# Moving T's copies to ScalarE and v's to VectorE in a fused FFT, soft-MoE and MLP kernel

## Chip, cores and metric

The kernel runs on one core of a Trainium2 chip. The metric is the device time of one execution in microseconds; the time of a kernel is the median of its runs.

## What is computed

The input x is 8 images of 3072 x 256. The reference takes the real part of a two-dimensional Fourier transform of each, flattens the images to 24576 rows, passes them through a soft mixture of 8 experts with 4 slots each, and then through a two-layer network.

```python
X = np.fft.fft(np.fft.fft(x, axis=1), axis=2).real
logits = x @ phi
d = softmax over the rows of logits
slot_out = relu((d.T @ x)[e] @ w1[e]) @ w2[e]
c = softmax over the slots of logits
x = c @ slot_out
h = x @ w_in
out = (s * relu(h)**2 + b) @ w_out
```

w_in and w_out arrive as float64 and are converted on the chip.

## The kernel before, in words

An image of 3072 rows is called a batch, and comes as three pages of 1,024 KB (`xb`), x0, x2 and x1, loaded in that order by `load_x` (L280). Pages of this size come from a ring of 15 (`page`), which later holds everything else that is large: the pages `xrt` of x for the weighted sums, tables (`ltab`, `htab_t`), logits (`lg`), raw and converted weights (`raw`, `wo`, `wi`, `whl`), `w1t` and `w2t`. A load waits until the last reader of the page it takes over is done. All loads are issued by SyncE in program order, so one that waits holds up those behind it.

The program is written for a manual schedule: each engine runs its instructions in the order in which the Python code emits them.

The first stage never forms the full transform. For each batch it computes V, x times a projected phi, transposed back, and then T, V times a 128-point table.
- `project` (L498) makes the projected phi, `phd`.
- `fold(b, op)` (L391) uses the symmetry of the transform: VectorE subtracts the mirrored page x2 from x0 into a page `fd`, and later adds it to x0 in place (L400, two instructions each). ScalarE copies one row that has no mirror (L395).
- `emit_v(n)` (L402): n = 2b is the even V, from x0 and `fd`, in 8 narrow matmuls (L413); n = 2b + 1 is the odd V, from x1 and x2, unfolded (L428). ScalarE copies V out of PSUM into `vts` (L419, L437). The last batch has an unfolded even V.
- `turn_v(n)` transposes it into `vq` (L446), and `turned_out(n)` copies that into `v` (L454): the even half by VectorE, the odd half by ScalarE.
- `emit_t(b)` (L458) multiplies v of one batch with the table into `tps` (L488) and puts eight small copies of it to `tt` on the list `late_t` (L496). For most batches six are ScalarE's and two VectorE's.

The loop over seven batches (L510) does, for batch b: start loads of x; fold (subtract); turned_out of batch b - 1; fold (add); odd V; T of batch b - 1; even V; all copies in `late_t`; transposes. The eighth batch follows, unfolded.

After the loop, `ORDER` (L287) gives the loads of a table in DRAM (s), x pages for the sums (r), and pages for tables (l, h). Then come the logits (L602), their exponentials and a second transform (L677), and the stage of weighted sums (L753 on TensorE), in which VectorE also converts w_out and w_in, four chunks each, in five steps per chunk (`double_steps`, L151 to L165), a maximum (L214, L231) and a split (L208). A raw page is free after the fifth step (L165). A string at L838 sets the order of the loads of x pages (x), w_out chunks (o) and w_in chunks (i). The experts follow (L962, L994), and then the two-layer network (L1158 to L1195), most of the run.

Of the kernel before, what the change touches and what calls it, by code (L numbers as in the profile page):

```python
# [13 lines left out]
ALU = mybir.AluOpType  # L14
# [19 lines left out]
def tile_fft2__then__softmoe__then__act_relu2(  # L34
# [18 lines left out]
    nc = tc.nc  # L53
    P = 128
    NS1 = 24
    B, S, D = 8, NS1 * P, xp.shape[-1]
# [40 lines left out]
    def page(shape, dt, name, among=9):  # L97
        k = [k for k, p in enumerate(pools[:among]) if p[2] < p[1]][-(len(pools) == 4)]
        pools[k][2] += 1
        return pools[k][0].tile(shape, dt, tag="page", name=name), k  # L100
# [4 lines left out]
    def drop(k):  # L105
        pools[k][2] -= 1
# [10 lines left out]
    def busy(eng, cost, after=0.0):  # L117
        at[eng] = max(at[eng], after, at["pe"]) + cost
# [165 lines left out]
    NX = 3 * B  # L284
    CR, BUDGET = 0.5, 3.9
    LEAD, TOL, LT, LX, HX = 14.0, 0.5, 0, 0, 1
    ORDER = 20 * "x" + "srllhh"  # L287
    tpool = tc.alloc_tile_pool(name="tpool", bufs=1)
    order = list(ORDER)

# [83 lines left out]
    with tc.tile_pool(name="xtp", bufs=1, side="right") as xtp, tc.tile_pool(name="vp", bufs=1, side="right") as vp, \  # L374
# [6 lines left out]
        late_t = []  # L381

        def turned(n, c, i, k, rev):

            v = xa[n][0][:, c, i, P - 1:P] if rev else xa[n][0][:, c, i, 0:1]
            sg = -1 if rev else 1
            return bass.AP(tensor=v.tensor, offset=v.offset, ap=[list(v.ap[0]), [sg * 2 * P, k], [sg, P]])

        fds = {}

        def fold(b, op):  # L391
            x0, x2 = xa[3 * b][0], xa[3 * b + 1][0]
            if op == ALU.subtract:
                fds[b] = page([P, 2, 8, P], F32, "fd")
                nc.scalar.copy(fds[b][0][:, :, 0, :], x0[:, :, 0, :])  # L395
            for c in range(2):
                v = x2[:, c, 7, P - 1:P]
                r = bass.AP(tensor=v.tensor, offset=v.offset, ap=[list(v.ap[0]), [-P, 7], [-1, P]])
                a = x0[:, c, 1:8, :]
                nc.vector.tensor_tensor(out=fds[b][0][:, c, 1:8, :] if op == ALU.subtract else a, in0=a, in1=r, op=op)  # L400

        def emit_v(n):  # L402
            b, part = divmod(n, 2)
            x0, x2, x1 = 3 * b, 3 * b + 1, 3 * b + 2
            vt = psv.tile([P, 4, P], F32, name="vt", bufs=2)

            if part == 0 and b < B - 1:
                d, dk = fds.pop(b)
                for c in range(2):
                    for h in range(2):  # L410
                        for j, t in enumerate((xa[x0][0], d)):
                            q = 64 * h + NE * j
                            nc.tensor.matmul(vt[q:q + NE], lhsT=phd[:, c, 0, NE * j:NE * j + NE], rhs=t[:, c, h::2, :],  # L413
                                             start=(c == 0), stop=(c == 1), tile_position=(0, q), skip_group_check=True)
                at["pe"] = max(at["pe"], x_at[x2] + 4.5) + 1.9
                for k in (xa[x0][1], dk):
                    drop(k)
                vts[n] = xtp.tile([P, 4, P], F32, name="vts", bufs=2)
                nc.scalar.copy(vts[n], vt)  # L419
                return  # L420
            if part == 0:
                todo_v = [(0, 0, 0, x0, 0, 4, 0), (1, 0, 0, x0, 1, 4, 0), (0, 1, 1, x2, 6, 3, 1), (1, 1, 0, x2, 7, 4, 1)]
            else:
                todo_v = [(0, 0, 0, x1, 0, 3, 0), (1, 0, 0, x1, 1, 3, 0), (0, 1, 0, x2, 0, 1, 1), (1, 1, 0, x1, 7, 2, 1),
                          (0, 1, 1, x1, 6, 1, 1)]
            for c in range(2):
                for m, (h, sg, o, pg, i, k, rev) in enumerate(todo_v):
                    nc.tensor.matmul(vt[64 * h:64 * h + 64, o:o + k, :], lhsT=phd[:, c, sg, :],  # L428
                                     rhs=turned(pg, c, i, k, rev), start=(c == 0 and m < 2), stop=(c == 1 and m >= len(todo_v) - 2),
                                     tile_position=(0, 64 * h), skip_group_check=True)  # L430
            at["pe"] = max(at["pe"], x_at[x1 if part else x2]) + (2.3 if part else 3.6)
            for pg in ((x1, x2) if part else (x0,)):
                drop(xa[pg][1])
            busy("act", 0.5)
            ns = 3 if part else 4
            vts[n] = xtp.tile([P, 4, P], F32, name="vts", bufs=2)
            (nc.scalar.copy if n < 2 * B - 1 else nc.vector.tensor_copy)(vts[n][:, 0:ns], vt[:, 0:ns])  # L437
# [11 lines left out]
        def turned_out(n):  # L449
            b, part = divmod(n, 2)  # L450
            bg, bq = divmod(b, NG)
            nk = 10 if part else 16
            vq = vqs.pop(n)
            (nc.scalar.copy if part and n < 2 * B - 4 else nc.vector.tensor_copy)(  # L454
                vs[bg][:, bq, :, 16 * part:16 * part + nk].rearrange("p (k j) n -> p j k n", j=4),
                vq.rearrange("p s (k j e) -> p j e (s k)", j=4, e=8)[:, :, :, 0:nk])

        def emit_t(b):  # L458
# [32 lines left out]
            for j in range(4):  # L491
                for c in range(2):
                    r = 64 * bg + NR * c
                    args = (tt[r:r + NR, :, bq, 8 * j:8 * j + 8],
                            t[NR * j:NR * j + NR, :, 64 * c:64 * c + 64].rearrange("p e k -> p k e"))
                    late_t.append(lambda args=args, dve=2 * j + c > 5 - b // (B - 2): (nc.vector.tensor_copy if dve else nc.scalar.copy)(*args))  # L496

        def project():  # L498
            pp = psv.tile([P, 2, 2, NE], F32, tag="tps", name="pp", bufs=2)
# [9 lines left out]

        for b in range(B - 1):  # L510
            pump_a()
            fold(b, ALU.subtract)
            if b:
                for n in range(2 * b - 2, 2 * b):
                    turned_out(n)
            fold(b, ALU.add)
            emit_v(2 * b + 1)
            if b:
                emit_t(b - 1)
            emit_v(2 * b)  # L520
            while late_t:
                late_t.pop(0)()
            turn_v(2 * b + 1)
            turn_v(2 * b)
            if b == 0:
                tp = psv.tile([P, P], F32, tag="tps", name="tp", bufs=2)
                nc.tensor.transpose(tp, f_sb, ident)
                nc.vector.tensor_copy(ft_sb, tp)
        for n in range(2 * B - 4, 2 * B - 2):
            turned_out(n)  # L530
        emit_v(2 * B - 2)
        while order:
            order_step()
        emit_t(B - 2)
# [300 lines left out]
        nc.sync.dma_start(out=w2t[e][:, c], in_=w2[e].rearrange("(p c) d -> p c d", p=P)[:, c])  # L835

    loads = {"o": iter(range(4)), "i": iter(range(4))}
    for c in "oxxoxxoxxoxxixxixxixix":  # L838
        if c == "x":
            todo.append((1, load_xr))  # L840
        else:
            k = next(loads[c])
            todo.append((3 - 2 * (k % 2), lambda k=k: wo_load(k), 1 - k % 2) if c == "o" else
                        (2 - k % 2, lambda k=k: wi_load(k), 1 - k % 2))
# [510 lines left out]
```

## Time and profile before

| | |
|---|---|
| median of 3 runs | 1443.61 us (1443.05 to 1444.81) |
| the profiled execution | 1445.31 us |
| its span | 1443.5 us |
| TensorE busy | 1374.8 us (95%) |
| VectorE busy | 1207.4 us (84%) |
| ScalarE busy | 1007.3 us (70%) |
| GpSimd busy | 237.0 us (16%) |
| DMA queue of the loads and stores | 110.78 MB |

The span is what the trace covers; the 1.8 us between it and the execution's own time lie around it. TensorE's 95% is an average over stages: of the 40 slices of the span, the first seven or so belong to the stages ahead of the two-layer network, and there its busy tenths are 6 to 9, with the granted clock at 7 to 9 tenths. A busy share says little about which engine sets the pace, so the rows to look at are those that tell what an engine waited for.

### The profile page before, as it was taken

How to read it: one execution, taken by the hardware profiler on the slowest of the kernel's cores; microseconds unless marked ns; L12 is line 12 of the kernel's file. 1: busy time of each engine (PE TensorE's matmuls, PEld its weight loads, DVE VectorE, ACT ScalarE, POOL GpSimd, SP SyncE). 2: the span in 40 equal slices, each digit the busy share in tenths (PEclk: the TensorE clock that was granted, in tenths of full speed). 3: DMA queues.
4: the chain of work that ended last, by engine and by line, in shares of the span. 5: the costliest groups of instructions: out<-in, count | busy, mean ns of one | idle time of the engine just before them, and what ended most of it. 6: DMA issues, size and time to landing. Idle time of an engine off the chain costs nothing.

```text
span 1443.5 us, 23041 instructions
## 1 busy us (share of the span) xinstructions
PE 1374.8 (95%) x8990; PEld 836.1 (58%) x8990; DVE 1207.4 (84%) x1523; ACT 1007.3 (70%) x1423; POOL 237.0 (16%) x287
## 2 busy tenths in 40 slices
PE   6667986999999999999999999999999999999998
PEld 4435653556666666666666666666666666666665
DVE  3446797599898989898989898989898989888886
ACT  2235431588787777787777787877777777777775
POOL 0030360012121212121212121111111111111110
PEclk8789997999999999999999999999999999999999
DMA  9955598210101010101010101010101010101001
GB/s 386 405 190 189 196 405 332 87 36 22 36 23 35 23 35 23 36 22 36 23 35 22 33 23 35 23 36 23 35 23 36 23 36 22 35 22 34 23 23 30
DMA packets 72460, 112.27 MB, mean 78 GB/s; under 512 B 34096, under 2 KB 59696, under 8 KB 64928
## 3 DMA queue, kind: packets, MB, share of 16 engines
q1 hardware_dynamic: 72320, 110.78, 22.3%
q8 instruction: 70, 1.15, 0.3%
q14 instruction: 38, 0.31, 0.1%
q0 software_dynamic: 32, 0.03, 0.0%
HBM read 78.50 MB, written 26.21 MB: 73 GB/s over the span
## 4 chain that ended last, share of the span: by engine, by line
PE 87%; DVE 7%; ACT 2%; issue 1%; DMA 1%; SPq 1%; POOL 0%; ACTq 0%; DVEq 0%; POOLq 0%
PE op L1192 45%; PE op L1195 23%; PE fhp L1158 11%; PE tps L488 2%; ACT tt L496 2%; PE vt L413 1%; DVE fd L400 1%; PE hp L677 1%; DVE whl L208 1%; DMA xb<-in_x_turned_dram 1%; PE ehp L962 1%; PE eop L994 1%; DVE tt L496 1%; SPq L1121 0%; DVE cm L615 0%
## 5 line engine op out<-in xcount | busy, mean ns | idle before, releaser
L1192 PE MATMUL op<-whl,rhl 128*128 128x512 f16 x3056 | 1020.7, 379 | 0.8 <-ACT rhl L1148 0.6
L1195 PE MATMUL op<-whl,rhl 128*128 128x256 f16 x3056 | 831.4, 273 | 0.0
L1163 ACT ACTIVATE r<-fhp,wsc 128x768 f32<-128x768 f32 (+1 forms) x513 | 461.4, 900 | 230.4 <-PE fhp L1158 229.2
L1164 DVE SCALAR_TENSOR_TENSOR r<-fhp,r 128x768 f32<-128x768 f32 (+1 forms) x513 | 489.1, 954 | 113.6 <-ACT r L1163 103.6
L1149 DVE TENSOR_TENSOR rhl<-r,rhl 128x768 f16<-128x768 f32 x511 | 506.8, 992 | 0.9 <-ACT rhl L1148 0.9
L1192 PEld LDWEIGHTS <-rhl 128*128 128x128 f16 x3056 | 298.9, 98 | 332.2 <-ACT rhl L1148 0.9
L1148 ACT CAST rhl<-r 128x768 f16<-128x768 f32 x511 | 420.2, 822 | 1.8 <-DVE r L1164 1.8
L1195 PEld LDWEIGHTS <-rhl 128*128 128x128 f16 x3056 | 299.0, 98 | 62.5 <-issue 0.3
L1211 POOL TENSOR_TENSOR ot<-ot,bias 128x256 f32<-128x256 f32 x189 | 137.7, 729 | 974.6 <-DVE ot L1209 974.6
L1158 PE MATMUL fhp<-ct,g 128*128 128x384 f16 x1024 | 250.5, 326 | 1.2 <-DMA g<-gs 0.8
L1158 PEld LDWEIGHTS <-g 128*128 128x128 f16 x1024 | 99.9, 98 | 69.0 <-issue 1.5
L1208 ACT ACTIVATE o<-op,small 128x256 f32<-128x256 f32 x189 | 89.8, 476 | 16.8 <-PE op L1195 16.8
L1209 DVE SCALAR_TENSOR_TENSOR ot<-op,small,o 128x256 f32<-128x256 f32 x191 | 91.2, 478 | 0.3
L496 DVE COPY tt<-tps 32x512 f32<-32x512 f32 x15 | 10.4, 694 | 53.2 <-ACT tt L496 53.1
L488 PE MATMUL tps<-f_sb,v 128*128 128x128 f32 x112 | 22.7, 386 | 29.6 <-DVE v L454 29.6
L753 PE MATMUL racc<-xrt,dh 128*64 128x256 f32 x384 | 45.8, 392 | 0.4 <-DVE dh L743 0.4
L419 ACT COPY vts<-vt 128x512 f32<-128x512 f32 x7 | 4.1, 585 | 56.3 <-PE vt L413 56.3
L753 PEld LDWEIGHTS racc<-xrt,dh 128*64 128x64 f32 x384 | 27.1, 140 | 21.7 <-issue 6.8
L488 PEld LDWEIGHTS tps<-f_sb,v 128*128 128x128 f32 x112 | 21.1, 290 | 31.8 <-issue 29.0
L428 PE MATMUL vt<-xb,phd 128*64 128x384 f32 (+3 forms) x176 | 24.8, 430 | 3.5 <-DMA xb<-in_x_turned_dram 3.5
L800 POOL TENSOR_TENSOR lg<-lg,rm 112x512 f32<-112x512 f32 x16 | 24.7, 1545 | 11.8 <-DVE rm L798 11.8
L496 ACT COPY tt<-tps 32x512 f32<-32x512 f32 x41 | 23.6, 575 | 3.7 <-PE tps L488 3.2
(249 smaller groups left out, 592.5 us busy)
## 6 DMA issues: line engine op xcount, KB each, us to landing
xb<-in_x_turned_dram SPq DMA_DIRECT2D x24, 1024.0 KB, 19.9
xrt<-in_x_pages_dram SPq DMA_DIRECT2D x24, 1024.0 KB, 8.3
out_dram<-ot SPq DMA_DIRECT2D x128, 128.0 KB, 1.7
w1t<-in_moe_w_dram SPq DMA_DIRECT2D x8, 1024.0 KB, 8.7
out_dram<-ot SPq DMA_DIRECT2D x128, 64.0 KB, 2.0
raw<-in_moe_w_out_dram SPq DMA_DIRECT2D x4, 1024.0 KB, 8.8
raw<-in_moe_w_in_dram SPq DMA_DIRECT2D x4, 1024.0 KB, 11.8
w2t<-in_moe_w_dram SPq DMA_DIRECT2D x4, 1024.0 KB, 13.8
```

Of the source, the lines that this page charges most:

```text
L496: late_t.append(lambda args=args, dve=2 * j + c > 5 - b // (B - 2): (nc.vector.tensor_copy if dve else nc.scalar.copy)(*args))
L753: nc.tensor.matmul(raccs[acc][64 * h:64 * h + 64, :], lhsT=dh[:, m, g].rearrange("p j e -> p (j e)"), rhs=xr[k][0][:, g, t, :], start=(sum ...
L1148: nc.scalar.copy(a, r2)
L1149: nc.vector.tensor_tensor(out=l, in0=r2, in1=a, op=ALU.subtract)
L1158: nc.tensor.matmul(hp[k * split][:, k, :].rearrange("p (s b m) -> p s b m", s=2, b=B), lhsT=g16[:, f * P:(f + 1) * P], rhs=c, start=True, ...
L1163: nc.scalar.activation(out=r[:, k], in_=hp[i][:, k], func=AF.Relu, scale=wsc[:, 2, p:p + 1])
L1164: nc.vector.scalar_tensor_tensor(out=r2[:, k], in0=hp[i][:, k], scalar=0.0, in1=r[:, k], op0=ALU.max, op1=ALU.mult)
L1192: nc.tensor.matmul(op.rearrange("p h d -> p (h d)"), lhsT=a, rhs=w.rearrange("p h d -> p (h d)"), start=(f == 0), stop=False)
L1195: nc.tensor.matmul(op[:, 0, :], lhsT=l, rhs=w[:, 0, :], start=False, stop=(f == NFC - 1))
L1208: nc.scalar.activation(out=o1, in_=op[:, 1, :], func=AF.Copy, scale=qv)
L1209: nc.vector.scalar_tensor_tensor(out=ot, in0=op[:, 0, :], scalar=qv, in1=o1, op0=ALU.mult, op1=ALU.add)
L1211: nc.gpsimd.tensor_tensor(out=ot, in0=ot, in1=bias, op=ALU.add)
```

## The change

Six things change, all ahead of the two-layer network.
- T's eight copies are all ScalarE's. They run in two groups of four: the first after the even V of the batch in which T is made, the second after the odd V of the next.
- Both halves of v are copied by VectorE.
- The row without a mirror is copied into `fd` by GpSimd, not ScalarE.
- Batch 0 is not folded; its even V is projected like the last batch's, and comes before its odd V.
- One more x page is loaded ahead of the table page (r twice in `ORDER`).
- In the string of loads, the first w_out chunk comes two x pages later, and the x pages between the w_in chunks are spread.

```diff
-    ORDER = 20 * "x" + "srllhh"
+    ORDER = 20 * "x" + "srrllhh"
...
             if op == ALU.subtract:
                 fds[b] = page([P, 2, 8, P], F32, "fd")
-                nc.scalar.copy(fds[b][0][:, :, 0, :], x0[:, :, 0, :])
+                nc.gpsimd.tensor_copy(fds[b][0][:, :, 0, :], x0[:, :, 0, :])
...
-            if part == 0 and b < B - 1:
+            if part == 0 and 0 < b < B - 1:
                 d, dk = fds.pop(b)
...
-            (nc.scalar.copy if part and n < 2 * B - 4 else nc.vector.tensor_copy)(
+            nc.vector.tensor_copy(
                 vs[bg][:, bq, :, 16 * part:16 * part + nk].rearrange("p (k j) n -> p j k n", j=4),
...
-                    late_t.append(lambda args=args, dve=2 * j + c > 5 - b // (B - 2): (nc.vector.tensor_copy if dve else nc.scalar.copy)(*args))
+                    late_t.append(lambda args=args: nc.scalar.copy(*args))
...
         for b in range(B - 1):
             pump_a()
-            fold(b, ALU.subtract)
             if b:
+                fold(b, ALU.subtract)
                 for n in range(2 * b - 2, 2 * b):
                     turned_out(n)
-            fold(b, ALU.add)
+                fold(b, ALU.add)
+            else:
+                emit_v(0)
             emit_v(2 * b + 1)
+            while late_t:
+                late_t.pop(0)()
             if b:
                 emit_t(b - 1)
-            emit_v(2 * b)
-            while late_t:
+                emit_v(2 * b)
+            for _ in range(4 * (b > 0)):
                 late_t.pop(0)()
             turn_v(2 * b + 1)
             turn_v(2 * b)
...
         emit_v(2 * B - 2)
+        while late_t:
+            late_t.pop(0)()
         while order:
             order_step()
...
-    for c in "oxxoxxoxxoxxixxixixxix":
+    for c in "xxoxxoxxoxxoxxixixixix":
```

Three places in the instruction order show what moves. The first is VectorE in the loop, from the fold of batch 2 to that of batch 3. Before:

```order
L400 TENSOR_TENSOR fd_277<-xb_149,xb_151 128x896 x2
L454 COPY v0_116<-vq_266 128x4x8x16
L400 TENSOR_TENSOR xb_149<-xb_149,xb_151 128x896 x2
L496 COPY tt_105<-tps_298 32x64x8 x2
L400 TENSOR_TENSOR fd_341<-xb_155,xb_157 128x896 x2
```

With the change:

```order
L400 TENSOR_TENSOR fd_267<-xb_149,xb_151 128x896 x2
L454 COPY v0_116<-vq_256 128x4x8x16
L454 COPY v0_116<-vq_252 128x4x8x10
L400 TENSOR_TENSOR xb_149<-xb_149,xb_151 128x896 x2
L400 TENSOR_TENSOR fd_331<-xb_155,xb_157 128x896 x2
```

The copies of `tps` to `tt` are gone from between one batch's folds and the next's, and the second copy of `vq` has come in.

The second is ScalarE over the same stretch (`vts` 128x384 is an odd V, 128x512 an even one). Before:

```order
L395 COPY fd_277<-xb_149 128x2x128
L454 COPY v0_116<-vq_262 128x4x8x10
L437 COPY vts_296<-vt_285 128x384
L419 COPY vts_316<-vt_307 128x512
L496 COPY tt_105<-tps_298 32x64x8 x6
```

With the change:

```order
L437 COPY vts_286<-vt_275 128x384
L496 COPY tt_105<-tps_228 32x64x8 x4
L419 COPY vts_310<-vt_301 128x512
L496 COPY tt_105<-tps_292 32x64x8 x4
L437 COPY vts_350<-vt_339 128x384
```

Four copies of the T made a batch ago (`tps_228`) now stand between the odd and the even V, and four of this batch's (`tps_292`) behind the even one.

The third is SyncE's queue around the first raw chunks of w_out, with the semaphores that each load waits for (DMAHW is an earlier load; DVE, PE, Activation and Pool are instructions of VectorE, TensorE, ScalarE and GpSimd). Before:

```order
L314 DMA xrt_756<-in_x_pages_dram 128x2048 [waits DMAHW5_49]
L147 DMA raw_1143<-in_moe2_w_out_dram 128x4x512 [waits DMAHW6_49,PE_49,Pool_49]
L314 DMA xrt_1145<-in_x_pages_dram 128x2048 [waits DMAHW7_49,PE_49]
L314 DMA xrt_1147<-in_x_pages_dram 128x2048 [waits DMAHW0_49]
L147 DMA raw_1149<-in_moe2_w_out_dram 128x4x512 [waits DMAHW1_49]
L314 DMA xrt_1187<-in_x_pages_dram 128x2048 [waits DMAHW2_49,PE_49,Pool_49]
```

With the change:

```order
L314 DMA xrt_1137<-in_x_pages_dram 128x2048 [waits DMAHW7_49,PE_49]
L147 DMA raw_1141<-in_moe2_w_out_dram 128x4x512 [waits DMAHW0_49]
L314 DMA xrt_1143<-in_x_pages_dram 128x2048 [waits DMAHW1_49]
L314 DMA xrt_1181<-in_x_pages_dram 128x2048 [waits DMAHW2_49,PE_49,Pool_49]
L147 DMA raw_1211<-in_moe2_w_out_dram 128x4x512 [waits DMAHW3_49,DMAHW0_49,DVE_49]
L314 DMA xrt_1232<-in_x_pages_dram 128x2048 [waits DMAHW4_49,PE_49]
L314 DMA xrt_1259<-in_x_pages_dram 128x2048 [waits DMAHW5_49,PE_49]
L147 DMA raw_1319<-in_moe2_w_out_dram 128x4x512 [waits DMAHW6_49,PE_49]
```

The second chunk's load (`raw_1149`, now `raw_1211`) waited for an earlier load alone; now it waits for VectorE too, for the fifth step on the first chunk, the last reader of the page that it takes over.

## Rows read from the trace of the kernel before

**Rows 1.** The table of stretches: us, busy (instructions) by engine, granted clock, DMA share, GB/s

```profile
30.00:40.00 10.00, 5.18 (x34) 4.48 (x30) 6.17 (x7) 3.37 (x7) 0.00 (x0) 0.77 1.01 420
...
21.02:105.77 84.75, 54.83 (x355) 35.00 (x354) 39.20 (x41) 27.50 (x54) 13.27 (x12) 0.82 0.82 318
...
155.70:239.40 83.70, 66.00 (x544) 37.82 (x544) 74.20 (x97) 25.44 (x52) 30.51 (x30) 0.92 0.86 338
```

**Rows 2.** The chain of waits from 33 us on: start us, us, what

```profile
33.66 2.09 DVE fd L400 x2
...
36.62 3.75 PE tps L488 x16
40.37 2.89 PE vt L413 x16
...
48.07 0.69 DVE tt L496
48.80 2.09 DVE fd L400 x2
...
125.67 1.18 PE lp L602 x18
```

**Rows 3.** The list of waits, 0 to 125 us: us in total, times, longest

```profile
DVE tt L496 <- ACT tt L496: 53.1, 7, 9.3
```

**Rows 4.** The timeline of TensorE: start us, us, instruction, idle before it

```profile
12.53 4.53 PE L428 MATMUL vt<-xb,phd 128*64 128x384 f32 x20 [3.55 <-DMA xb<-in_x_turned_dram]
...
21.02 2.38 PE L428 MATMUL vt<-xb,phd 128*64 128x384 f32 x20
24.17 2.02 PE L488 MATMUL tps<-f_sb,v 128*128 128x128 f32 x16 [0.77 <-DVE v L454]
26.12 0.62 PE L413 MATMUL vt<-xb,phd 128*32 128x512 f32 x1
...
27.98 0.55 PE L446 MATMUL vq<-ident,vts 128*128 128x128 f32 x3
...
29.42 2.38 PE L428 MATMUL vt<-xb,phd 128*64 128x384 f32 x20
36.62 3.75 PE L488 MATMUL tps<-f_sb,v 128*128 128x128 f32 x16 [4.82 <-DVE v L454]
```

**Rows 5.** Groups of instructions by form, 21 to 106 us: busy, mean ns, idle before

```profile
L496 ACT COPY tt<-tps 32x512 f32<-32x512 f32 x32 | 18.4, 576 | 0.4
```

**Rows 6.** The timelines of TensorE and VectorE at the stage's end

```profile
105.77 3.65 PE L428 MATMUL vt<-xb,phd 128*64 128x512 f32 x16
111.26 2.05 PE L488 MATMUL tps<-f_sb,v 128*128 128x128 f32 x16 [1.83 <-DVE v L454]
...
110.11 1.09 DVE L454 COPY v<-vq 128x512 f32<-128x512 f32 x2
...
118.44 0.56 DVE L437 COPY vts<-vt 128x384 f32<-128x384 f32 x1
```

**Rows 7.** The timelines of VectorE and GpSimd, copies on GpSimd

```profile
77.25 4.88 DVE L400 TENSOR_TENSOR fd<-xb 128x896 f32<-128x896 f32 x2
...
78.61 2.57 POOL L547 COPY ltab<-ltab 64x2048 f32<-64x2048 f32 x1
...
249.71 0.39 POOL L948 COPY sel<-sel_sb 128x256 f32<-128x256 f32 x1 [4.01 <-DMA sel_sb<-in_sel_dram]
```

**Rows 8.** The timeline of VectorE in the stage of weighted sums

```profile
166.99 1.22 DVE L165 SCALAR_TENSOR_TENSOR wo<-raw,wo 128x1024 uint32<-128x1024 uint32 x1
...
172.78 0.68 DVE L151 TENSOR_SCALAR wo<-raw 128x1024 uint32<-128x1024 uint32 x1
...
184.16 1.53 DVE L151 TENSOR_SCALAR wo<-raw 128x1024 uint32<-128x1024 uint32 x1
```

**Rows 9.** Issues of raw loads at 167.89 and 182.82: KB, us to landing

```profile
raw<-in_moe_w_out_dram SPq DMA_DIRECT2D x1, 1024.0 KB, 5.4
...
raw<-in_moe_w_in_dram SPq DMA_DIRECT2D x1, 1024.0 KB, 14.7
```

More of the change, by code (lines that the diff above doesn't have):

```diff
@@ L837, in tile_fft2__then__softmoe__then__act_relu2 @@
     loads = {"o": iter(range(4)), "i": iter(range(4))}
-    for c in "oxxoxxoxxoxxixxixxixix":
+    for c in "xxoxxoxxoxxoxxixixixix":
         if c == "x":
```

## The prediction

> **What bounds the kernel now.** I first split the run by stage with the table of stretches [rows 1]. The three-page loop that builds V and T for seven of the eight images (call an image a batch) takes 84.75 us, and in it TensorE is busy 54.83 us, VectorE 39.20 and ScalarE 27.50, at a granted clock of 0.82. No engine fills this stage. The x pages do not set it either: at the 420 GB/s of one stretch [rows 1] a page of 1,024 KB takes 2.50 us, so a batch of three takes 7.5, and six batches take 45.
>
> Next I read the chain of waits inside the loop [rows 2]. From one fold on VectorE (33.66) to the next (48.80) one batch takes 15.14 us, and the links run in a ring: fold, v, T's matmuls (3.75), V's matmuls (2.89), ScalarE's copy of V, ScalarE's six copies of T, VectorE's two copies of T (the last at 48.07), and only then the next fold. The list of waits names the link that closes the ring: VectorE sat idle 53.1 us, seven times, before its copies of T, until ScalarE's copies ended [rows 3]. VectorE works in order, so the fold of the next batch, which needs nothing from T, stands behind them.
>
> TensorE pays twice: it idles while the ring goes round, and after 4.82 us idle the T matmuls take 3.75 us, where after 0.77 us idle the same sixteen records took 2.02 [rows 4], near the ratio of 1.2 to 2.4 GHz.
>
> The stages after the loop are not touched in their arithmetic. In the stage of weighted sums and weight conversion VectorE is busy 74.20 of 83.70 us [rows 1], so that stage is bound by VectorE.
>
> **The loop.** VectorE loses its two copies of T and gains the odd half of v, which ScalarE did before. Its work in a batch is then the two folds, 2.09 together [rows 2], the two v copies, 1.09 [rows 6], and the two in-place folds, taken as the same 2.09: 5.3 us, and no copy of T stands in its queue. ScalarE has eight copies of T at 0.576 [rows 5] and two of V, which have as many elements in a partition or fewer, so no more than the same: 5.8 us. Each batch's T is copied in two groups of four, 2.3 us a group, one behind the even V copy of its own batch and one behind the odd V copy of the next; neither group delays a copy that TensorE waits for, because 2.02 us of T and 1.86 of even V (26.12 to 27.98), or the transposes and 2.38 of odd V, lie between those copies [rows 4].
>
> What is late next is TensorE itself. Batch 1 of the run before shows its period at the full clock without the ring: from one odd V at 21.02 to the next at 29.42 is 8.40 us, of which 0.77 is the wait for v in front of T [rows 4]. That wait goes: v is ready about 1.2 us after TensorE starts its odd V, and odd V takes 2.38. Where the fold takes over a page from the V before it (batches 2 and 3 in the instruction order), it starts when that V ends (27.98), 1.4 us ahead of the odd V (29.42), so v ends some 1.8 us into it: still hidden. So the period is 8.40 - 0.77 = 7.63 us, just over the 7.5 of the x pages. Six batches take 45.8 in place of the 84.75 from 21.02 to 105.77 [rows 4, 6]: **-39.0 us**. Bounds: 45.0 if the pages set the pace (-0.8), 50.4 if the wait for v stays (+4.6).
>
> **The first batch.** The order no longer folds batch 0, so TensorE starts on its even V as soon as the second page is in, about 2.5 us before the 12.53 at which the third let odd V start [rows 4]. Unfolded V takes 3.65 us at full clock, as it does for the last batch [rows 6], and up to 7.3 at half. From 10.0 that ends at 17.3 at worst; then odd V 2.38, transposes and copies 1.3: 21.0. At best batch 1 starts with its third page at 12.53 + 3 x 2.50 = 20.0. I take 21.0, so **0**, since batch 1 starts at 21.02 now; bounds -1.0, and +2.1 if odd V runs at half clock too (4.53, as in the run before [rows 4]).
>
> **The tail of the stage.** From the last batch's even V (105.77) to the first logits matmul (125.67) [rows 2, 6] is 19.90 us. TensorE idles there 1.83 us before T [rows 6] and again before the last transposes, because VectorE still holds copies of T. With these gone, even V 3.65, T 2.05 and odd V 2.38 follow each other, 8.1 us, and from VectorE's copy of the last V (118.44) to the logits (125.67) nothing changes, 7.23: 15.3. **-4.6 us**. Bounds: 0 to -4.6; ScalarE's twelve remaining copies of T (6.9 us) end 11.2 us into the tail, before its next input at about 11.5.
>
> **GpSimd's copy of the first fold row.** Now six copies of 128 x 256, which took 0.39 us in the one such copy of this run [rows 7]. I take **0**: GpSimd has nothing else there, and even V needs the copy about 4 us later. Against it: the pair of folds that ran beside GpSimd's copies of a table took 4.88 us, not 2.09, while one of those copies took 2.57 [rows 7]. If each copy holds up its fold for its own length, six cost 2.3 us, my upper bound; VectorE has 7.63 - 5.3 = 2.3 us of slack in each batch to hide 0.39. The Trainium skill, page "SBUF — State Buffer", section "Who interferes with whom", has the rule: a VectorE instruction with two SBUF inputs and a GpSimd instruction that reads SBUF shut each other out for the whole instruction. By that rule without the slack the sum would be 2.3 us worse; the slow folds agree with the rule.
>
> **w_out two pages later.** The logits stage now starts at 82.1, and needs one table page, queued behind two page loads where one stood before. The x pages end at about 12.5 + 21 x 2.5 = 65; that table's source, two pages and the table itself end at about 75. Hidden, with 7 us to spare. The raw weights fare differently. The second chunk's raw page is now the one that the first gives back: its load waits for VectorE's fifth step on the first chunk. That step ends at 168.2 and the second chunk's first step starts at 172.78 [rows 8]: 4.6 us. The one load issued onto idle queues in this stage landed in 5.4 us, the slowest, behind a full queue, in 14.7 [rows 9]. With an allowance of 0.2 to issue, and idle queues, which is what the order leaves there, VectorE stalls **+1.0 us**; bounds 0 and +10.3, and the row nearest is the 5.4. The third chunk's load follows it with two pages between, so it lands about 5.4 + 3 x 2.50 = 12.9 us after that step, and is used 16 us after it (184.16 [rows 8]): 0, with 3 us to spare. Later ones have more.
>
> **Sum.** -39.0 - 4.6 + 1.0 = -42.6 us, against the profiled execution's 1445.31 (span 1443.5): 1402.7. The median of the runs is 1443.61, 1.7 less; so **1401.0 us**. With the lower bounds (-0.8, -1.0, no stall -1.0) 1398; with the three small upper ones together (+4.6, +2.1, +2.3) 1410, with the slowest landing alone (10.3 for 1.0) 1410.
>
> **Rivals.**
> *The clock falls again.* If TensorE still waits in each batch long enough for the clock to drop to 1.2 GHz, T takes 3.75 for 2.02 and even V 2.89 [rows 2] for 1.86: +2.7 a batch, +16, 1417. For it: the mean clock is 0.82 now, and 7.63 is near the pages' 7.5. Against: the waits left are under 1 us, and after 1.83 us idle T still took 2.05 [rows 6]. The Trainium skill ("TensorE: Matmul & The Clock Gate", section "HAM oscillation — how this bites in real kernels") warns of loops whose gaps throttle the array each time; the 3.75 agrees, but such gaps are what this change takes out.
> *The gain is given back to DMA.* The weighted-sum stage starts 43.6 us earlier, and the queues have that much less time for its pages. Its 83.70 us have a DMA share of 0.86 [rows 1], so 11.7 us are idle. If page waits push 8 pages (20 us) into it, 20 - 11.7 = 8.3 us come back: 1409. For it: loads there wait for pages to come free. Against: between 65 and 112 us 47 us of transfers fit, and 12 pages, the tables and one chunk need about 40.
> *Slower: every conversion waits for its load.* If not one but all seven later chunks' raw pages hang on the chunk before, VectorE, which bounds that stage, stalls at each by its load less 4.6 us. At the slowest landing seen, 14.7 [rows 9], that is 7 x 10.1 = 71 in place of the +1.0: 1471. It decides from landings of 10.8 us on, where 7 x 6.2 eats the 43.6. Against: in the instruction order only the second chunk's load hangs on the chunk just before it.
> *The change does not do what it says:* the order shows no copy of T left on VectorE inside the loop, so hardly.
>
> **Chances.** Forecast 0.78 (own range 1397 to 1408), DMA 0.10, clock 0.08, slower 0.03, no change 0.01. The range 1397 to 1412 holds the forecast and the DMA case and leaves out the rest and some misses, under 2 in 10. A measurement of this kernel tells 0.2%, 2.9 us, from no change: faster 0.96, same 0.01, slower 0.03.
>
> **What would show it.** Right: odd V matmuls every 7.6 us; VectorE's idle before copies of T gone; T near 2.0 us each batch; first logits matmul near 82 us; weighted sums 43 us earlier and as long as before plus 1 us, with one gap of VectorE before the second chunk. Wrong: T still at 3.7 us, a period over 9 us, logits waiting for their table, or VectorE gaps at each chunk.

## Result, and the profile after

The changed kernel takes **1404.2 us** (median of 4 runs, 1403.81 to 1404.26), the kernel before beside it 1443.33 (4 runs): a ratio of 0.9727, 95% interval 0.971 to 0.9744, so 39.1 us less. The forecast was 1401.0, the range 1397 to 1412. The profiled execution took 1404.26 us with a span of 1402.5, 41.0 below the span of before.

From the timelines of both kernels the 41.0 us split so (b2 is the start of the odd V of batch 2; from that batch on each kernel repeats its own pattern):

| stretch | before | after | difference |
|---|---|---|---|
| start to b2 | 29.42 | 28.45 | -0.97 |
| b2 to the last batch's even V (five batches) | 76.35 | 37.93 | -38.42 |
| from there to the first logits matmul (tail) | 19.90 | 16.54 | -3.36 |
| logits and second transform, to the first htp | 30.05 | 29.90 | -0.15 |
| weighted sums, to the copy of rsb | 83.19 | 84.09 | +0.90 |
| experts, to the first gp | 28.65 | 29.59 | +0.94 |
| the rest | 1175.94 | 1176.00 | +0.06 |

The table of stretches for the changed kernel, with the columns of [rows 1]: the five batches, the tail, and the weighted sums.

```profile
28.45:66.38 37.93, 36.39 (x296) 22.09 (x296) 25.16 (x29) 27.93 (x51) 8.25 (x9) 1.00 1.02 420
66.38:82.92 16.54, 13.55 (x137) 8.46 (x136) 5.78 (x14) 11.84 (x25) 4.83 (x6) 0.94 0.70 230
112.82:196.91 84.09, 67.57 (x544) 38.28 (x544) 73.75 (x96) 25.56 (x52) 30.89 (x30) 0.92 0.90 361
```

In the loop TensorE is now busy 36.39 of 37.93 us at a granted clock of 1.00, which is 2.4 GHz, in place of 54.83 of 84.75, over six batches, at 0.82 [rows 1]. It is the bound, with the DMA share at 1.02 right beside it. The timeline of TensorE, against [rows 4]:

```profile
19.23 4.07 PE L428 MATMUL vt<-xb,phd 128*64 128x384 f32 x20 [2.98 <-DMA xb<-in_x_turned_dram]
23.22 2.05 PE L488 MATMUL tps<-f_sb,v 128*128 128x128 f32 x16
...
28.45 2.38 PE L428 MATMUL vt<-xb,phd 128*64 128x384 f32 x20
30.75 2.05 PE L488 MATMUL tps<-f_sb,v 128*128 128x128 f32 x16
...
36.03 2.38 PE L428 MATMUL vt<-xb,phd 128*64 128x384 f32 x20
38.34 2.05 PE L488 MATMUL tps<-f_sb,v 128*128 128x128 f32 x16
```

From b2 on odd V follows every 7.58 us, and T takes 2.05 with no wait ahead of it. Batch 1 is the exception: 2.98 us of idle time for its page, then 4.07 for an odd V that otherwise takes 2.38. The list of waits over the first 125 us has no line any more for copies of T on VectorE (L496), which stood at 53.1 us [rows 3]. What VectorE waits for in the loop is TensorE and the pages (engine, what waits, for what: us in total, times, longest):

```profile
DVE fd L400 <- PE vt L413: 7.7, 2, 5.5
DVE v L454 <- PE vq L446: 7.5, 4, 4.5
...
DVE fd L400 <- DMA xb<-in_x_turned_dram: 3.3, 4, 1.4
```

The tail of the changed kernel, timelines of TensorE and then of ScalarE, against [rows 6]:

```profile
74.25 1.35 PE L446 MATMUL vq<-ident,vts 128*128 128x128 f32 x7
76.19 1.16 PE L464 MATMUL tpa<-f_sb,v 128*128 128x128 f32 x8 [0.58 <-DVE v L454]
77.27 1.12 PE L477 MATMUL tpb<-f_sb,v 128*32 128x64 f32 x64
80.60 2.26 PE L183 MATMUL warm<-dd,ones 128*128 128x512 f32 x4 [2.21 <-ACT tt L483]
82.92 4.93 PE L608 MATMUL lp<-tt,ltab 64*64 64x128 f32 x130
```

```profile
70.74 7.04 ACT L496 COPY tt<-tps 32x512 f32<-32x512 f32 x12
77.79 2.16 ACT L469 COPY tt<-tpa 32x128 f32<-32x128 f32 x8
79.97 0.58 ACT L483 COPY tt<-tpb 64x512 f32<-64x512 f32 x1
```

ScalarE's twelve copies of T run until 77.78, its eight small copies of `tpa` wait behind them (where nothing holds them up, in e3 below, they start 0.75 us behind the first of `tpa`'s matmuls, which here would be at 76.94), and TensorE's next matmuls, which only keep it warm, wait 2.21 us for ScalarE's last copy and then take 2.26.

VectorE in the weighted sums, against [rows 8]: the fifth step of the first chunk, and the first step of the second with the one new gap.

```profile
124.09 1.23 DVE L165 SCALAR_TENSOR_TENSOR wo<-raw,wo 128x1024 uint32<-128x1024 uint32 x1
...
130.81 0.69 DVE L151 TENSOR_SCALAR wo<-raw 128x1024 uint32<-128x1024 uint32 x1 [0.85 <-DMA raw<-in_moe_w_out_dram]
```

### The profile page after: what moved, and what is told of

It is laid out like the page before. It is cut to its first block, busy times and chain, and to the rows that moved or that the text cites. A ratio compares the mean times of both kernels' runs of the same rounds, so it can differ in the third digit from the quotient of the medians.

```text
span 1402.5 us, 23032 instructions
## 1 busy us (share of the span) xinstructions
PE 1367.2 (97%) x8990; PEld 829.8 (59%) x8990; DVE 1191.8 (85%) x1510; ACT 1011.3 (72%) x1425; POOL 240.9 (17%) x293
## 4 chain that ended last, share of the span: by engine, by line
PE 87%; DVE 4%; DMA 1%; ACT 1%; issue 0%; SPq 0%; POOL 0%; DVEq 0%; ACTq 0%; POOLq 0%
PE op L1198 46%; PE op L1201 23%; PE fhp L1164 12%; PE racc L759 1%; PE hp L683 1%; DMA w1t<-in_moe_w_dram 1%; DVE cm L621 1%; PE ehp L968 1%; PE eop L1000 1%; PE dps L744 0%; SPq L1127 0%; DMA raw<-in_moe_w_out_dram 0%; PE op L1195 0%; DVE wo L165 0%; DVE r L1170 0%
## 5 line engine op out<-in xcount | busy, mean ns | idle before, releaser
L496 ACT COPY tt<-tps 32x512 f32<-32x512 f32 x56 | 32.3, 576 | 0.7
L428 PE MATMUL vt<-xb,phd 128*64 128x384 f32 (+3 forms) x192 | 27.8, 436 | 3.4 <-DMA xb<-in_x_turned_dram 3.0
L806 POOL TENSOR_TENSOR lg<-lg,rm 112x512 f32<-112x512 f32 x16 | 24.7, 1544 | 10.5 <-DVE rm L804 10.5
L428 PEld LDWEIGHTS vt<-xb,phd 128*64 128x64 f32 x192 | 16.0, 144 | 13.6 <-issue 11.1
L437 ACT COPY vts<-vt 128x384 f32<-128x384 f32 (+1 forms) x9 | 4.5, 502 | 26.7 <-PE vt L428 26.7
L400 DVE TENSOR_TENSOR fd<-xb 128x896 f32<-128x896 f32 x12 | 13.0, 1122 | 11.0 <-PE vt L413 7.7
L788 POOL TENSOR_TENSOR lg<-et,lg 112x512 f16<-112x512 f32 x16 | 20.2, 1261 | 0.8 <-ACT lg L791 0.8
```

## The experiments

All runs, with the stretches of the table above in us. Each kernel ran beside the kernel before, whose median lay between 1442.62 and 1443.33.

| run | median | start to b2 | five batches | tail | sums | experts |
|---|---|---|---|---|---|---|
| the change | 1404.2 | 28.45 | 37.93 | 16.54 | 84.09 | 29.59 |
| e1_ring_back | 1447.06 | 29.54 | 76.07 | 20.11 | 84.25 | 29.53 |
| e2_t_dve_spread | 1408.96 | 29.74 | 37.93 | 19.96 | 84.17 | 29.44 |
| e3_no_spread | 1403.45 | 30.20 | 37.92 | 14.80 | 84.13 | 29.28 |
| e4_t_act_alone | 1416.08 | 27.42 | 52.56 | 14.79 | 83.17 | 29.11 |
| e5_warm_gap | 1403.51 | 28.53 | 37.93 | 15.94 | 84.08 | 28.47 |
| e6_fold0 | 1403.15 | 27.97 | 37.93 | 15.64 | 84.23 | 28.53 |
| e7_w_out_early | 1402.99 | 29.91 | 37.93 | 15.64 | 83.29 | 29.14 |
| e8_fd_scalare | 1404.52 | 28.81 | 37.90 | 16.49 | 84.08 | 29.67 |
| e9_two_edits | 1402.43 | 28.54 | 38.54 | 14.79 | 83.17 | 29.03 |
| e10_three_undone | 1401.79 | 28.35 | 37.94 | 14.80 | 83.19 | 29.04 |
| e11_warm_slot | 1402.41 | 28.71 | 37.93 | 14.40 | 83.20 | 29.08 |
| e12_change_again | 1404.40 | 28.46 | 37.93 | 16.78 | 84.25 | 29.19 |

The medians of the kernel before lie 0.7 us apart, and its single executions up to 3.8 (1439.79 to 1443.63, beside e9 to e12), so differences of about a microsecond between medians say little; the stretches tell more.

### The ring: its place, or the engine?

**e1_ring_back**, the changed kernel with

```diff
-                    late_t.append(lambda args=args: nc.scalar.copy(*args))
+                    late_t.append(lambda args=args, dve=2 * j + c > 5 - b // (B - 2): (nc.vector.tensor_copy if dve else nc.scalar.copy)(*args))
...
-            for _ in range(4 * (b > 0)):
+            for _ in range(len(late_t)):
```

> The changed kernel with the last two copies of each T back on VectorE (three for the last T made in the loop) and all eight copies behind the even V again, as before the change; everything else as changed. My theory, the ring: the two copies stand between one batch's folds and the next's again, so a batch runs from the end of even V through ScalarE's copy of V and six of T (0.65 + 3.5 us), two copies on VectorE (1.3), the fold (2.1) and the v copies (1.1) to the next T, which leaves TensorE idle some 5 us and at half clock: 14 to 15 us a batch in place of 7.6, so about 1443 us, all of the gain gone. Rival A, that the gain is the odd half of v leaving ScalarE, the unfolded first batch and the order of the loads: these are kept, so the time stays under 1425. Rival B, that spreading the copies over two batches is what matters and the engine is not: also about 1443, so the next run is needed beside this one.

1447.06 us (1444.91 to 1447.95, ratio 1.0025, 1.0016 to 1.0035): all of the gain is gone, and 3.9 us more against the kernel before beside it, with the five other parts of the change in place. The five batches take 76.07 us, where they took 76.35: with the ring closed, the move of v, the fold row's copy and the rest give the loop next to nothing, which rules out rival A. Of the 3.9 us the profiles show 1.9, in the sums (1.06) and the experts (0.88), on which more below; the rest stays open. The old wait is back, in the list of waits of the first 125 us and then in the timeline of TensorE, in front of T:

```profile
DVE tt L496 <- ACT tt L496: 57.7, 7, 10.3
```

```profile
37.04 3.78 PE L488 MATMUL tps<-f_sb,v 128*128 128x128 f32 x16 [5.13 <-DVE v L454]
...
52.09 3.68 PE L488 MATMUL tps<-f_sb,v 128*128 128x128 f32 x16 [5.13 <-DVE v L454]
```

**e2_t_dve_spread**, the changed kernel with the first of the two edits alone, so that VectorE's two copies come with the odd V of the next batch.

> The changed kernel with the last two copies of each T back on VectorE (three for the last T made in the loop), but with the copies spread over two batches as changed, so that VectorE's two stand behind the odd V of the next batch and have no fold waiting just behind them. Theory, that the place in VectorE's queue and not its 1.2 us of work closed the ring: they wait for two ScalarE copies that end some 1.8 us after that odd V, while T and even V keep TensorE busy for 3.9 us more, so the period stays at 7.6 us; in the tail ScalarE has five copies fewer, and up to 2.2 us of TensorE's wait for it may go: 1402 to 1405 us. Rival, that VectorE must not hold copies of T at all: 14 us a batch, 1440 or more. Rival, that VectorE's own work is short (5.3 us of 7.6): its 1.2 us more would add 1 us a batch, about 1410.

1408.96 us (1407.44 to 1409.96). The five batches take 37.93 us, to the hundredth what they take without any copy of T on VectorE. So neither the engine nor its 1.4 us of work closed the ring by itself. Nor did what stands behind those copies by itself, although I had expected that no fold would follow them here: in VectorE's queue the next batch's fold stands right behind them in both runs (the timeline of VectorE in e1, then in e2).

```profile
47.39 1.40 DVE L496 COPY tt<-tps 32x512 f32<-32x512 f32 x2 [8.40 <-ACT tt L496]
48.82 2.10 DVE L400 TENSOR_TENSOR fd<-xb 128x896 f32<-128x896 f32 x2
```

```profile
49.10 1.40 DVE L496 COPY tt<-tps 32x512 f32<-32x512 f32 x2 [0.91 <-ACT tt L496]
50.53 2.09 DVE L400 TENSOR_TENSOR fd<-xb 128x896 f32<-128x896 f32 x2
```

What differs is which T they copy. In e1 it is the T just made, whose first six copies ScalarE makes only behind the even V that follows this T, and VectorE, with the fold behind, waits 8.40 us for them. In e2 it is the T made one round of the loop earlier, and the wait is at most 0.94 us in these five batches.

Of the rivals, 14 us a batch and 1 us a batch are both out; the 1410 of the latter came close by another way, and my own 1402 to 1405 missed. Most of the loss lies in the tail, 19.96 for 16.54, where I had expected a gain; the start of this profile is 1.29 us longer, and the logits stage 1.08. In the tail VectorE's last three copies, waiting for ScalarE's, stand ahead of its copy of the last V again, and TensorE waits for that (the timeline of VectorE, then that of TensorE):

```profile
76.46 2.11 DVE L496 COPY tt<-tps 32x512 f32<-32x512 f32 x3 [1.54 <-ACT tt L496]
78.60 0.56 DVE L437 COPY vts<-vt 128x384 f32<-128x384 f32 x1
```

```profile
79.21 0.67 PE L446 MATMUL vq<-ident,vts 128*128 128x128 f32 x3 [3.01 <-DVE vts L437]
```

This is a second, shorter chain of the same kind, and that the tail term of the prediction rests on taking it away is shown by this run.

### The spread, and what else opens the loop

**e3_no_spread**, the changed kernel with the second of the two edits of e1 alone: all eight copies on ScalarE, behind the even V of their batch.

> The changed kernel with all eight copies of T on ScalarE, but all behind the even V of their own batch, not in two groups. Theory: they end 5.3 us after that even V, and the next copy that ScalarE owes, of the odd V, is wanted only when TensorE is through with T and even V, 7.3 us after: nothing waits, the period stays at 7.6 us, and in the tail ScalarE has four copies fewer, which may give back 1 to 2 us: 1402 to 1405 us. Rival, that the spread carries part of the gain: TensorE waits for ScalarE's copy of V by up to 2.3 us a batch, 1418 or so.

1403.45 us (1402.37 to 1404.11), five batches in 37.92: with all copies on ScalarE the spread gives the loop nothing. e2 and e3 each keep one of the two edits of e1, and in each the ring is open: it takes both, copies on VectorE and copies of the T just made, to close it. The tail is 14.80, 1.74 shorter than in the change, as ScalarE enters it with four copies fewer; the median shows less of that, since the start of this profile is 1.75 longer.

**e4_t_act_alone**, the kernel before with one line changed, the first edit of the diff of e1 the other way round: T's eight copies all ScalarE's.

> The kernel before with one edit: all eight copies of T on ScalarE, all else as it was, the odd half of v and the first fold row on ScalarE too. Theory: the ring through VectorE is open, but a second, shorter one takes its place on ScalarE: from the end of even V its copy of V, eight of T and the fold row take 5.7 us, and only then comes its copy of the odd half of v, 0.7, for which the next T waits; TensorE is done with odd V after 3.4 us, so it idles about 3 us a batch, long enough for its clock to fall in some batches: 10.6 to 12.5 us a batch, 1418 to 1431 us. Rival, that taking T off VectorE is the whole gain: 1404 to 1406. Rival, that the gain is in the other edits: 1440 or more.

1416.08 us (1414.95 to 1418.83; ratio 0.9818, 0.9802 to 0.9835), 10.5 us a batch, just under the low end. The second ring is where it was expected; the list of waits from 27 to 80 us:

```profile
PE tps L488 <- ACT v L454: 10.2, 4, 2.6
```

The timeline of ScalarE shows it: the copies of T, the fold row and only then the odd half of v, for which T waits.

```profile
38.44 4.70 ACT L496 COPY tt<-tps 32x512 f32<-32x512 f32 x8
43.17 0.41 ACT L395 COPY fd<-xb 128x256 f32<-128x256 f32 x1
43.60 0.43 ACT L454 COPY v<-vq 128x320 f32<-128x320 f32 x1
```

The clock fell in one of those waits only: T took 3.31 us once, after 2.52 us idle, and 2.02 to 2.05 in the other four batches, after 2.51 to 2.64.

### The first batch

**e5_warm_gap**, the changed kernel with, behind batch 0's transposes,

```diff
+                w0 = psv.tile([P, 4 * P], F32, tag="tps", name="w0", bufs=2)
+                for _ in range(2):
+                    keep_busy(w0, 4 * P)
```

> The changed kernel with two matmuls on a table, whose result is not used, put behind the transposes of batch 0, in the gap of 3 us in which TensorE waits for the first page of batch 1. In the changed kernel the odd V behind that gap took 4.07 to 4.53 us and the T behind it up to 2.63, where later batches take 2.38 and 2.05. Theory: the gap makes TensorE's clock fall, the x pages do not hold it back there; with the gap filled by 2.2 us of work odd V takes 2.38, batch 2 starts 1.7 to 2.5 us sooner, and the whole by as much, since later batches run at TensorE's pace of 7.58 us: 1402 to 1402.5. Rival: the loop runs behind the x pages, which take 7.5 us a batch, so what is won there is lost again in waits for pages within the loop: 1404.

1403.51 us (1402.39 to 1405.59). The timeline of TensorE:

```profile
16.29 1.88 PE L183 MATMUL w<-dd,ones 128*128 128x512 f32 x4
19.67 2.37 PE L428 MATMUL vt<-xb,phd 128*64 128x384 f32 x20 [1.50 <-DMA xb<-in_x_turned_dram]
...
28.53 1.94 PE L428 MATMUL vt<-xb,phd 128*64 128x384 f32 x14 [1.26 <-DMA xb<-in_x_turned_dram]
```

The mechanism is as thought: with the gap filled odd V takes 2.37. The size is the rival's: batch 2 then waits 1.26 us for a page, and starts at 28.53, no sooner than in the profile of the change. That is sooner than in e1, e2, e3 and e7, where odd V of batch 1 took 4.53; all five batches behind it ran at 7.58 without a wait.

**e6_fold0**, the changed kernel with batch 0 folded and its even V behind its odd V, as in the kernel before.

> The changed kernel with batch 0 folded again, its even V narrow and behind its odd V, as before the change; the rest as changed. My prediction put the unfolded first batch at 0. Theory now: it costs something, since unfolded V is done before the pages of batch 1 are there and the gap lets the clock fall; in the run with T on ScalarE alone, which folds batch 0, batch 1 ran at full clock and batch 2 started at 27.4 us, against 28.45 to 30.2 in the three runs without the fold. So this one starts batch 2 by 1 to 2.5 us sooner: 1402 to 1403. Rival: the first batch's fold holds back VectorE's fold of batch 1 and the start is the same or later: 1404 to 1406.

1403.15 us (1402.51 to 1404.06). Batch 2 starts at 27.97, and TensorE has hardly a gap ahead of batch 1 (0.12 us). In the six profiles with a folded first batch (before, e4, e6, e9, e10, e11) batch 2 starts at 27.42 to 29.42, in the mean at 28.4; in the seven without fold or filler (the change twice, e1, e2, e3, e7, e8) at 28.45 to 30.20, in the mean at 29.3. So the unfolded first batch gains nothing, and costs some 0.9 us by these means. Single profiles of the two kinds overlap, so this size is less sure than the others here.

### The order of the loads

**e7_w_out_early**, the changed kernel with

```diff
-    for c in "xxoxxoxxoxxoxxixixixix":
+    for c in "oxxoxxoxxoxxixxixixxix":
```

> The changed kernel with the string of loads as before the change (first w_out chunk first); all else as changed. The second chunk's raw page then waits for no step of the first. Theory, from my term of +1.0: VectorE's gap ahead of the second chunk (0.85 us) goes, and SyncE's queue, which stood behind that load from 112 to 125 us, goes on earlier, so the load of w1t lands sooner and the first matmuls of the experts take 2.8 us instead of 3.6: 1.5 us less in all, 1402.5. Rival, that the later w_out chunk is itself part of the gain because x pages are then sooner for the weighted sums: those wait for pages instead, 1405 to 1409.

1402.99 us (1402.73 to 1404.13). The gap ahead of the second chunk is gone; the same two instructions of VectorE:

```profile
125.17 1.22 DVE L165 SCALAR_TENSOR_TENSOR wo<-raw,wo 128x1024 uint32<-128x1024 uint32 x1
...
130.97 0.68 DVE L151 TENSOR_SCALAR wo<-raw 128x1024 uint32<-128x1024 uint32 x1
```

The weighted sums take 83.29 us. Over all kernels this is the cleanest of the numbers: 84.08 to 84.25 in the eight profiles with the new string, and 83.17 to 83.29 in the six with the old one (before, e4, e7, e9, e10, e11). The second half of the theory fell: the experts still took 29.14 us, so the loads of w1t are not what makes them longer (see the last section).

### GpSimd's copy

**e8_fd_scalare**, the changed kernel with `nc.scalar.copy` for the fold row's copy (L395).

> The changed kernel with the copy of the row without a mirror back on ScalarE; all else as changed. Theory: GpSimd's copies lengthened two pairs of folds by 0.2 us, hidden under TensorE, so the time stays at 1404 +- 0.7 and those folds take 2.09; ScalarE has 0.4 us more a batch out of 1.8 free. Rival: ScalarE's copy waits for an x page ahead of its copy of odd V, and delays that: 0.4 us or more a batch, 1406.5 or more.

1404.52 us (1402.74 to 1404.67), no difference, as the theory had it. The change's timelines of GpSimd and VectorE at that copy in batch 3, then VectorE's of e8 there:

```profile
14.59 0.40 POOL L395 COPY fd<-xb 128x256 f32<-128x256 f32 x1 [11.75 <-PE vt L428]
...
34.84 1.32 POOL L395 COPY fd<-xb 128x256 f32<-128x256 f32 x1 [6.21 <-PE vt L413]
```

```profile
34.81 2.29 DVE L400 TENSOR_TENSOR fd<-xb 128x896 f32<-128x896 f32 x2 [2.24 <-PE vt L413]
...
40.78 2.09 DVE L400 TENSOR_TENSOR fd<-xb 128x896 f32<-128x896 f32 x2 [0.68 <-DMA xb<-in_x_turned_dram]
```

```profile
35.17 2.10 DVE L400 TENSOR_TENSOR fd<-xb 128x896 f32<-128x896 f32 x2 [2.44 <-PE vt L413]
```

Beside a fold the copy took 1.32 us in place of 0.40, and the pair of folds 2.29 in place of 2.09 or 2.10. The Trainium skill, page "SBUF — State Buffer", section "Who interferes with whom", says that a VectorE instruction with two SBUF inputs contends with a GpSimd instruction that reads SBUF, for a port pair that is locked by one of them at a time. The copy's 0.92 us more, nearly the 1.04 of one of the pair's two instructions, agree with that; the folds lost 0.20, half of the copy's own 0.40, which no run here explains. VectorE's slack hides it.

### Fewer edits, and a better kernel

**e9_two_edits**, the kernel before with two lines changed:

```diff
-            (nc.scalar.copy if part and n < 2 * B - 4 else nc.vector.tensor_copy)(
+            nc.vector.tensor_copy(
...
-                    late_t.append(lambda args=args, dve=2 * j + c > 5 - b // (B - 2): (nc.vector.tensor_copy if dve else nc.scalar.copy)(*args))
+                    late_t.append(lambda args=args: nc.scalar.copy(*args))
```

> The kernel before with two edits: all eight copies of T on ScalarE, behind the even V of their batch, and both halves of v on VectorE. Nothing else of the change: batch 0 folded, the first fold row on ScalarE, the old order of loads, no spreading. Theory: these two open both rings (VectorE's, and the shorter one on ScalarE that T on ScalarE alone left), and the other four parts give nothing or cost 1 to 2 us each; the period is 7.6 us, the tail 14.8 as in the runs without the spread, the weighted sums 83.2 as before: 1398 to 1401 us, some 4 us under the changed kernel. Rival, that the other parts are needed (the fold row's copy on ScalarE, the spread): a period of 8 us or more, 1406 or more.

1402.43 us (1401.66 to 1403.79; ratio 0.9723, 0.9709 to 0.9736), a little over the range expected, which I had taken from spans (its span is 1400.0). On the same chip the whole change took 1404.40 (1402.77 to 1404.85). The two lines give all that the change gives; the 2.0 us between the two are less than the 2.9 that I set as measurable, but the stretches say where they lie: 1.99 in the tail, 1.08 in the sums, against 0.61 in the loop, which runs at 7.7 us a batch. The cause of that stays open; e10, which differs from e9 only in GpSimd's copy and the second x page ahead of the table, has 37.94 in the loop. The second x page was not tested by itself.

**e10_three_undone**: the changed kernel with the edits of e3, e6 and e7 together.

> The changed kernel with three of its parts undone together: no spreading of T's copies, batch 0 folded, the old string of loads. What stays: T on ScalarE, v on VectorE, the fold row on GpSimd, two x pages ahead of the table. Theory, from the runs that undid one each: 1.7 us in the tail, 1 to 1.6 at the start, 0.9 in the weighted sums add up, as they lie in different stages: 1399 to 1401. Rival, that they do not add, since what the start wins is lost to waits for x pages: 1402 or more.

1401.79 us (1400.74 to 1402.11), 2.6 less than the change beside it, span 1399.8 against 1402.6: the tail gives 1.98 of the 2.8 in the span, the sums 1.06, the start and the experts 0.26, and the logits take 0.47 back. The median lies just over the range expected, which again came from spans.

**e11_warm_slot**: e10 with, ahead of the logits,

```diff
-        keep_busy(psv.tile([P, 4 * P], F32, tag="vt", name="warm", bufs=2), 4 * P)
-        keep_busy(psv.tile([P, 4 * P], F32, tag="vt", name="warm", bufs=2), P)
+        keep_busy(psv.tile([P, 4 * P], F32, tag="tps", name="warm", bufs=2), 4 * P)
+        keep_busy(psv.tile([P, 4 * P], F32, tag="tps", name="warm", bufs=2), P)
```

> As the run before with those three parts undone, and the matmuls that keep TensorE warm ahead of the logits put in another PSUM buffer (that of T, free earlier). Theory: TensorE waited 1.4 to 2.2 us there for ScalarE's last copy, only because the warming matmuls took over its buffer; with the wait gone they run in the gap and the logits start as soon as VectorE's last copy to tt ends: 0.3 to 0.7 us less than the run before. Rival: the logits wait for that ScalarE copy themselves, no difference.

1402.41 us (1402.07 to 1402.88), not better than e10. The tail is 0.40 shorter, as expected, but the second half of the logits gives it back. The table of stretches for the logits' second half, in e11 and then in e10 (the first numbers behind the length are TensorE's, the clock is the third from the end):

```profile
87.90:92.70 4.80, 4.73 (x106) 4.54 (x105) 3.75 (x6) 2.79 (x5) 0.00 (x0) 0.64 0.82 336
```

```profile
87.90:91.40 3.50, 3.40 (x104) 3.00 (x104) 2.97 (x5) 2.21 (x4) 0.00 (x0) 1.00 0.83 337
```

The same hundred matmuls take 4.73 us at a granted clock of 0.64, and 3.40 at 1.00. So e10 is the best of these kernels, by a margin over e9 and e11 that these runs do not settle.

**e12_change_again**: the changed kernel.

> The changed kernel itself, beside the others on one chip: 1403.5 to 1404.5 us. In its profile TensorE's clock falls in the gap ahead of batch 1 as in the other runs with an unfolded first batch; if the odd V of batch 1 takes 4.53 and not 4.07, batch 2 starts up to 1 us later than in the profile seen first.

1404.40 us, as in the first runs of it. Batch 2 starts at 28.46; the gap ahead of batch 1 and the long tail are there again.

## Why the prediction was right, and where it was off

The case forecast as the likeliest is the one that came. The profiled execution took 1404.26 us where the sum said 1402.7. The other 1.6 us of the 3.2 between forecast and median are from the step from that execution to the median: that of before lay 1.7 to 2.0 over its median, that of after at it.

- **The loop**, -39.0: right, and shown. Start and loop together gave -39.4 (the last batch's even V starts at 66.38, not 105.77). The period is 7.58 for 7.63. (The 84.75 us are six batches, as the sum has it, not the seven of the prediction's first paragraph. From the odd V of batch 1 on they came to 47.15 us, -37.6, since batch 1 alone took 9.22; the rest of the -39.4 is its earlier start.) The link named, VectorE's copies of T ahead of the next fold, is shown by e1, e2 and e3: put back there as copies of the T just made, they cost all the gain; as copies of the T before it, in the same place ahead of the fold, they cost the loop nothing. What the prediction did not see is the second ring: without the move of v the loop is left with a shorter one on ScalarE, worth 14.0 us (e4 with 52.56 against e9 with 38.54, one edit apart).
- **The first batch**, 0: the size was right by luck, the working was not. The first V began at 8.70 and not at 10.0, and took 5.81 us for its even and odd part together, so at full clock and not at half. Batch 1 started at 19.23, earlier than even my lower bound of 20.0, since the pages landed sooner than in the profile of before (the third at 11.61 and not 12.40). But the gap ahead of batch 1 let the clock fall, which I had not reckoned with, and 1.7 us came back.
- **The tail**, -4.6: this is the term that was mis-sized; it measured -3.4. The step that failed is that "from VectorE's copy of the last V (118.44) to the logits (125.67) nothing changes, 7.23", with ScalarE's twelve copies ending "11.2 us into the tail, before its next input at about 11.5". They ended 11.4 us in, but the next input was ready 10.6 us in, and from VectorE's copy of the last V (74.44) to the logits took 8.48. Without the backlog (e3) it is 6.74. The slower clock of the warming matmuls is part of it: they took 2.26 us at a granted clock of 0.56, where e3 has 1.35 at 1.00. The step took the end of ScalarE's copies to be hidden and left no room for it; the range did not count the tail's own bound of 0 either.
- **GpSimd's copy**, 0: right, by e8; the interference is there, at 0.2 us a pair.
- **w_out two pages later**, +1.0: right. The load landed 5.43 us after its issue, right behind the step that it waited for (forecast 5.4), the gap is 0.85, the stage 0.90 longer, and e7 takes it away.
- **Not in the sum**: +0.9 in the experts, where identical matmuls met the clock's return sooner or later (last section); no part of the change touches them.

Of the rivals, the fall of the clock in every batch did not come, nor did waits for pages in the weighted sums: beside the one gap the stage is as long as before. A gap at every chunk did not come, since only one load hangs on the chunk just before it.

## What to carry to other kernels

Where an engine works in order, look at what an instruction waits for and at what stands behind it, not only at its own cost: two copies of 0.7 us, with the next batch's fold behind them, cost 38 us where they waited for work of the same round of the loop, and nothing where that work was a round old. After a ring is opened, go once more round the engines that took over its work, and look at the stage's end, where a backlog that the steady loop hides comes due. And take a change of many parts apart: here two lines carry the gain, and three of the other parts each cost about a microsecond.

## What the hardware showed

The clock of TensorE came and went in ways worth 1 to 2 us at three places, and identical code there differed by as much. Ahead of batch 1, odd V took 3.75 to 4.53 us after 2.94 to 3.28 us of idle time in seven profiles, and 2.37 after 1.50 us of it, behind filling work (e5). In e4 some 2.5 us of idle time ahead of T cost the clock in one batch of five. And the experts' stage, untouched by every edit, took 28.47 to 29.67 us, as the clock came back sooner or later after 11.8 to 13.2 us without matmuls. The table of stretches from 203 to 206 us, in the changed kernel, then in e6:

```profile
203.00:206.00 3.00, 3.00 (x17) 0.60 (x16) 0.00 (x0) 0.00 (x0) 0.70 (x1) 0.50 0.41 158
```

```profile
203.00:206.00 3.00, 3.00 (x25) 0.68 (x21) 0.46 (x2) 0.57 (x1) 0.56 (x2) 0.79 0.19 71
```

The granted clock is 0.50 (1.2 GHz) in the one and 0.79 in the other, and the first sixteen matmuls of the experts took 3.64 and 2.75 us. In all fourteen profiles these sixteen start 6.18 us behind the copy of rsb and take 2.70 to 3.64 us, and the rest of the stage takes 25.76 to 26.03: nearly all of the difference is theirs. I had first put this 0.9 to the loads of w1t; e7, and e6 with the same order of loads as the change, speak against it, and so does the start, which is the same in all.
